# Three reads of the attention bias move from the sync engine's DMA queue to GpSimd's

## The chip, the cores and the metric

The kernel runs on one core of a Trainium2 chip. Its time is the device time of one execution in microseconds (us). The engines are PE (TensorE, matrix products), DVE (VectorE), ACT (ScalarE), POOL (GpSimd) and SP (SyncE, which here only issues DMAs). Each engine takes its instructions in program order; they wait for one another through semaphores. A DMA is issued by an engine's queue, and it "lands" when its last byte is there and its semaphore says so.

## What is computed

An attention with a bias that depends on positions, then two MLP blocks. Only the bias matters here; cut from the reference:

```
B, H, S, D = 4, 8, 576, 64
rel = pos[:, None] - pos[None, :]
x = (log1p(abs(rel)) / log1p(maximum(pos[:, None], 1.0)))[..., None]
bias = maximum(x @ w1 + b1, 0.0) @ w2            # (S, S, H): the same for every batch
scores = scale * q @ k.T + bias.transpose(2, 0, 1)[None]
attn = exp(scores - max) / (sum + 1e-9)
out = attn @ v                                   # then the MLP blocks
```

The bias is a 576 x 576 matrix for each of the 8 heads; row i depends on |i - j| alone, apart from the divisor.

## The kernel before

**Stages.** The kernel first computes the bias of all heads (about the first 53 us), then does the attention in 16 units (`UNITS`: four pairs of heads times four batches, `hp` and `b`), then the MLP blocks.

**The bias stage.** A strip z is 16 rows of the bias for all 8 heads, so 128 partitions. There are 36 strips, done in the order `ORDER`: strips 16 to 23, then 8 to 15, then 0 to 7, then 24 to 35; y is the place in that order. For each strip, `units` makes four hidden tiles m from L (a relu of shifted and scaled logs; most on DVE at L335, some on ACT at L333), `sums` multiplies them with the weights on PE (L347), and `finish` writes the result with its mirror image into a tile o (ACT at L354, DVE at L356). `store` (L368) then sends o to a scratch buffer `scr` in DRAM, 591 numbers a row. Reading `scr` back with a row pitch that is shorter by one turns this into the bias matrix. Strips 0 to 23 go with one store each. Strips 24 to 35 go in groups of 3 and 1, for the first two heads only at first (the other heads follow in the attention); the second head's stores of strips 32 to 34 and 35 are issued from ACT, all others from SP.

**The reads.** `read(k)` loads rows 128k to 128k+127 of the first two heads from `scr` into the tile `bias`. For even k a row is put in a turned order, so `turned` takes two DMAs (L262 and L263); for odd k it is one (L376). `read(4)` loads the last 64 rows with two (L276). `READ` says after which place y each is issued: read 2 after y = 20, read 0 after y = 27, read 1 after y = 29, read 3 after y = 32, read 4 after y = 35. Read k needs strips 8k to 8k+7.

**Who uses them.** The first attention unit works on nine blocks of 128 rows in the order `FIRST`: add 0, add 1, add 2, add 5, add 3, add 6, add 4 (DVE, L714: scores plus bias, with the row minimum). Add n takes read n mod 5: add 0 and 5 read 0, add 1 and 6 read 1, add 2 read 2, add 3 read 3, add 4 read 4. S n is the score product on PE (L708), exp n on ACT (L728), T n the transposes on PE (L734), hi n and lo n their split on ACT (L117) and DVE (L120).

**POOL.** Between 5 us and 51 us POOL has nothing to do in this stage. Behind the bias stage stands a first, tiny copy (`GATE`, L114, into w), which waits for the last strip's hidden tile; then come the low half of K for the second head (kl), the split of the next unit's q, of v, and some fills.

**Semaphores of DMAs.** As built, every DMA from SP or ACT counts on one of eight semaphores, named DMAHW0 to DMAHW7 in the rows of the program below, and waits for the DMA that used the same one before it. Those issued from POOL count on DMASW0 and following.

Of the kernel before, what the change touches and what calls it, by code (L numbers as in the profile page):

```python
# [100 lines left out]
def block_kernel(  # L101
# [6 lines left out]
    act, dve, pool, pe, sp = nc.scalar, nc.vector, nc.gpsimd, nc.tensor, nc.sync  # L108
# [146 lines left out]
    def rows(h, i, n):  # L255

        f = 16 + h * PITCH + i * (H * PITCH - 1)
        return scr[f:f + n * (H * PITCH - 1)].rearrange("(r c) -> r c", r=n)[:, :2 * PITCH].rearrange("r (h j) -> r h j", h=2)[:, :, :S]

    def turned(dst, src):  # L260

        sp.dma_start(out=dst[..., 64:], in_=src[..., :512])  # L262
        sp.dma_start(out=dst[..., :64], in_=src[..., 512:])  # L263

    def load_bias(hp, z):

        if hp not in bias:
            new_bias(hp)
        if z < 2:
            t = bias[hp][:, 5 * z:5 * z + 4]  # L270
            src = rows(2 * hp, 0, 512)[:, z].rearrange("(n p) j -> p n j", p=128)
            turned(t[:, ::2], src[:, ::2])
            sp.dma_start(out=t[:, 1::2], in_=src[:, 1::2])
        else:
            for h in range(2):
                sp.dma_start(out=bias[hp][64 * h:64 * h + 64, 4], in_=rows(2 * hp, 512, 64)[:, h])  # L276
# [4 lines left out]
    with ExitStack() as c:  # L281
# [21 lines left out]
        for f in (load_q, load_k):  # L303
# [9 lines left out]
            out=W.rearrange("p (g h) -> p g h", h=8), in0=w8.unsqueeze(1).to_broadcast([128, 4, 8]), in1=ind.unsqueeze(2).to_broadcast([128, 4, 8]), op=ALU.mult,  # L313
# [56 lines left out]
        def read(k):  # L370
            if k == 4:
                load_bias(0, 2)
                return
            t, src = bias[0][:, k::5], rows(0, 128 * k, 128)
            if k % 2:
                sp.dma_start(out=t, in_=src)  # L376
            else:
                turned(t, src)

        def finish(z, pts):  # L380
            l, r, n = reach(z)
            if z < FULL:
                t = stg.tile([128, 591], F32, name="o")
            else:
                if z % 4 == 0:
                    spare[z // 4] = M["spare"].tile([128, 4 * 591], F32, name="o")
                t = spare[z // 4][:, 591 * (z % 4):][:, :591]
            left, right = t[:, :l + 1][:, ::-1], t[:, l:]
            for o, pt in pts:
                scaled(EV[ORDER.index(z)][0], z, (right if z < 18 else left)[:, o], pt)  # L390
            if z < 18:
                scaled(EV[ORDER.index(z)][1], z, left[:, 1:], pts[0][1][:, 1:l + 1])
            else:
                scaled(EV[ORDER.index(z)][1], z, right[:, 1:], pts[0][1][:, 1:r])
            if z < FULL:
                store(z, 1, t)
            else:

                for n, at in GROUPS:
                    if z % 4 == at:  # L400
                        for h in range(2):
                            store(z + 1 - n, n, spare[z // 4][:, 591 * (at + 1 - n):591 * (at + 1)], h)
                if z % 4 == 3:
                    M.setdefault("held", []).append(lambda: store(z - 3, 4, spare[z // 4]))
            for k in READ.get(ORDER.index(z), ()):
                read(k)
# [5 lines left out]
        for y, z in enumerate(ORDER):  # L412
# [19 lines left out]
            if y == QK[2]:  # L432

                KH, KL = (qkp.tile([128, 2, S + 64], F32R, name=n) for n in ("kh", "kl"))
                k = raw[0].pop("k")
# [549 lines left out]
    def T_groups(b):  # L985
        return [g_T(b, j) for j in ([4] if b % 2 == 0 else []) + [0, 1, 2, 3]]
# [4 lines left out]
    with ExitStack() as c:  # L991
# [98 lines left out]
        for k in range(4):  # L1090
            for m in range(3):
                src = wiv[:, k, 1024 * m:1024 * m + 1024] if m < 2 else wov[:, k]
# [263 lines left out]
    t = {b: T_groups(b) for b in range(1, B)}  # L1356
# [83 lines left out]
```

## Time and profile before

| | us |
|---|---|
| median of 3 runs | 946.3 (946.25 to 948.57) |
| the profiled execution's own time | 945.16 |
| its span, first to last instruction | 943.4 |
| PE busy in the span | 922.5 (98%) |
| DVE busy | 720.6 (76%) |
| ACT busy | 494.9 (52%) |
| POOL busy | 425.1 (45%) |

The time is that of one core. PE is busy for nearly the whole span, so the stretches in which it isn't are where anything else can count: the bias stage and the first attention unit, in the first 70 us. Of the views, the chain of waits is the work that ended last, followed back from the end; the timeline shows instructions in order of time, with the idle time of the engine before one in brackets and what ended it; the table by stretches gives each engine's busy time in one.

### The profile page before, as it was taken

The numbers are of one execution on the slowest core, as the hardware profiler recorded it, in microseconds if no ns is written. First come the engines' busy times: TensorE is split into PE (matmuls) and PEld (weight loads), VectorE is DVE, ScalarE is ACT, GpSimd is POOL, SyncE is SP. The second block draws the span as 40 slices with busy tenths as digits, with TensorE's granted clock in tenths as the row PEclk, the third lists the DMA queues.
The fourth block names the chain that finished last, engine by engine and source line by source line (L and its number), as shares of the span: only waits on it lengthen the run. The fifth ranks groups of instructions, "written<-read, shape, count | busy, mean of one in ns | idle before, by whom it ended". The sixth has DMA issues, their size and how long they took to land.

```text
span 943.4 us, 16015 instructions
## 1 busy us (share of the span) xinstructions
PE 922.5 (98%) x5681; PEld 805.8 (85%) x5681; DVE 720.6 (76%) x1433; ACT 494.9 (52%) x1108; POOL 425.1 (45%) x555
## 2 busy tenths in 40 slices
PE   7889999999999999999999999999999999999998
PEld 2269999999999888888888888888888998989996
DVE  7988999999889687885779798979765656455452
ACT  8979999999998754322222222223132635253340
POOL 0068788978999543332224333433300524133251
PEclk9999999999999999999999999999999999999999
DMA  6878847757563561212122333233222000001001
GB/s 230 283 234 258 270 137 214 236 162 226 158 206 85 177 196 31 70 33 89 61 68 92 123 99 122 88 124 99 101 67 104 23 1 23 24 0 58 1 34 67
DMA packets 57983, 110.23 MB, mean 117 GB/s; under 512 B 10032, under 2 KB 21040, under 8 KB 57648
## 3 DMA queue, kind: packets, MB, share of 16 engines
q1 hardware_dynamic: 57504, 108.64, 36.1%
q8 instruction: 45, 0.74, 0.3%
q10 hardware_dynamic: 400, 0.58, 0.2%
q14 instruction: 34, 0.28, 0.1%
HBM read 71.37 MB, written 28.38 MB: 106 GB/s over the span
## 4 chain that ended last, share of the span: by engine, by line
PE 91%; DVE 5%; POOL 1%; DMA 1%; issue 1%; ACT 1%; DVEq 0%; SPq 0%; POOLq 0%; ACTq 0%
PE psh L124 21%; PE psy L124 21%; PE psa L124 10%; PE s L708 8%; PE PB L797 8%; PE psa L1284 6%; PE pt L734 6%; PE psa L1266 5%; DVE m L335 4%; PE pt L487 1%; PE OB L803 1%; PE s L744 1%; PE pt L347 1%; DVE ct L714 0%; DMA L<-in_c_log_dram 0%
## 5 line engine op out<-in xcount | busy, mean ns | idle before, releaser
L124 PE MATMUL psh<-blk,w1h 128*128 128x512 f32 (+1 forms) x640 | 151.5, 368 | 0.0
L176 POOL TENSOR_TENSOR cvl<-cvl,cvt 128x512 f32<-128x512 f32 x44 | 56.9, 1293 | 206.6 <-DVE cvt L173 179.0
L655 ACT ACTIVATE hh<-psh 128x512 fp32r<-128x512 f32 (+1 forms) x80 | 44.1, 553 | 194.4 <-PE psh L124 193.2
L124 PEld LDWEIGHTS psh<-blk,w1h 128*128 128x128 f32 x640 | 113.3, 188 | 20.8 <-DVE blk L120 0.2
L714 DVE CUSTOM_DVE_ANT_0 ct<-s,bias 128x576 f32<-128x576 f32 x144 | 107.0, 752 | 16.6 <-PE s L708 7.1
L728 ACT ACTIVATE a<-ct,sm 128x576 f32<-128x576 f32 x144 | 112.2, 779 | 3.2 <-DVE sm L714 2.6
L1087 DVE TENSOR_TENSOR x_sb<-psy,x_sb 128x512 f32<-128x512 f32 x144 | 97.2, 683 | 9.1 <-PE psy L124 8.6
L656 DVE SCALAR_TENSOR_TENSOR hl<-psh,hh 128x512 fp32r<-128x512 f32 (+1 forms) x80 | 50.5, 632 | 56.5 <-ACT hh L655 56.5
L124 PE MATMUL psy<-w2h,hh 128*128 128x512 f32 x288 | 90.2, 394 | 0.1
L124 PE MATMUL psy<-w2l,hh 128*128 128x512 f32 x288 | 88.9, 390 | 0.0
L124 PE MATMUL psy<-w2h,hl 128*128 128x512 f32 x288 | 88.8, 389 | 0.0
L734 PE MATMUL pt<-ident,a 128*128 128x128 f32 x576 | 84.9, 273 | 0.3 <-DVE at0l L120 0.3
L124 PE MATMUL psh<-blk,w1l 128*128 128x512 f32 (+1 forms) x320 | 79.0, 368 | 0.0
L708 PE MATMUL s<-kh,q 128*128 128x288 f32 x320 | 72.0, 314 | 3.1 <-DVE sm L714 2.4
L734 PEld LDWEIGHTS pt<-ident,a 128*128 128x128 f32 x576 | 68.6, 141 | 1.1 <-DVE at0l L120 0.6
L708 PE MATMUL s<-kl,q 128*128 128x288 f32 x320 | 65.8, 295 | 0.0
L124 PEld LDWEIGHTS psh<-blk,w1l 128*128 128x128 f32 x320 | 56.8, 189 | 10.0
L124 PEld LDWEIGHTS psy<-w2l,hh 128*128 128x128 f32 x288 | 54.0, 188 | 11.5
L124 PEld LDWEIGHTS psy<-w2h,hl 128*128 128x128 f32 x288 | 54.0, 188 | 11.5
L177 POOL TENSOR_TENSOR cvw<-cvl,cvw 128x512 f32<-128x512 f32 x44 | 59.9, 1362 | 3.5
L124 PEld LDWEIGHTS psy<-w2h,hh 128*128 128x128 f32 x288 | 52.6, 188 | 9.9 <-issue 0.2
L120 DVE TENSOR_TENSOR at0l<-pt,at0h 128x512 fp32r<-128x512 f32 (+1 forms) x80 | 49.5, 619 | 5.6 <-ACT at0h L117 5.2
(202 smaller groups left out, 2173.5 us busy)
## 6 DMA issues: line engine op xcount, KB each, us to landing
r<-in_moe_w_ch_dram SPq DMA_DIRECT2D x32, 512.0 KB, 4.8
k<-in_k_dram SPq DMA_DIRECT2D x16, 640.0 KB, 5.4
q<-q SPq DMA_DIRECT2D x64, 144.0 KB, 2.7
scr<-o SPq DMA_DIRECT2D x24, 295.5 KB, 3.3
v<-in_v_dram SPq DMA_DIRECT2D x16, 384.0 KB, 3.5
q<-in_q_dram SPq DMA_DIRECT2D x16, 288.0 KB, 3.7
bias<-scr SPq DMA_DIRECT2D x8, 576.0 KB, 5.7
bias<-scr SPq DMA_DIRECT2D x8, 512.0 KB, 5.0
```

The source lines that it names most:

```text
L120: (eng or dve).tensor_tensor(out=o, in0=i, in1=hi.bitcast(F32), op=ALU.subtract)
L124: pe.matmul(ps, lhsT=w, rhs=x, start=start and j == 0, stop=stop and j == len(terms) - 1)
L176: pool.tensor_tensor(out=T["l"], in0=T["l"], in1=T["t"].bitcast(F32), op=ALU.mult)
L177: pool.tensor_tensor(out=T["w"], in0=T["l"], in1=T["w"], op=ALU.add)
L656: dve.scalar_tensor_tensor(out=hl[:, f, :n], in0=ps[:, :n], scalar=0.0, in1=hh[:, f, :n].bitcast(F32), op0=ALU.max, op1=ALU.subtract)
L708: pe.matmul(s[:, x, :288], lhsT=w, rhs=m[:, 288 * x:288 * x + 288], start=j == 0, stop=j == len(prs) - 1)
L714: dve.tensor_tensor_reduce(out=ct, in0=s[:, :, :288], in1=bias[UNITS[u][0]][:, n].rearrange("p (a b) -> p a b", a=2), scale=-0.125, scalar ...
L728: act.activation(weights(n), ct.rearrange("p a b -> p (a b)"), AF.Exp, scale=-1.0, bias=mt, accum_out=SU[u % 2][:, n:n + 1])
L734: pe.transpose(PA[k % 2][:, j], e[:, 128 * j:128 * j + 128], ident)
L797: pe.matmul(d, lhsT=w, rhs=m, start=q == 0, stop=q == len(terms) - 1)
L1087: dve.tensor_tensor(out=x_sb[:, t], in0=ps, in1=x_sb[:, t], op=ALU.add)
L1284: pe.matmul(ps[:, z, :288], lhsT=v, rhs=w[:, 288 * z:288 * z + 288], start=(q == 0), stop=(q == len(terms) - 1))
```

## The change

`turned` takes the queue as an argument, and `read` hands POOL's queue to reads 0, 1 and 2 and SP's to read 3. Read 4 goes through `load_bias` and stays on SP. The later loads of bias, which call `turned` too, keep SP.

```diff
-    def turned(dst, src):
+    def turned(dst, src, q=sp):
-        sp.dma_start(out=dst[..., 64:], in_=src[..., :512])
-        sp.dma_start(out=dst[..., :64], in_=src[..., 512:])
+        q.dma_start(out=dst[..., 64:], in_=src[..., :512])
+        q.dma_start(out=dst[..., :64], in_=src[..., 512:])
...
             t, src = bias[0][:, k::5], rows(0, 128 * k, 128)
+            q = pool if k < 3 else sp
             if k % 2:
-                sp.dma_start(out=t, in_=src)
+                q.dma_start(out=t, in_=src)
             else:
-                turned(t, src)
+                turned(t, src, q)
```

What this does to the order, in two places. First POOL's queue, after its opening fills (L318): the five DMAs of reads 2, 0 and 1, in that order, ahead of the copy of the gate (into w) and of kl.

```order
 L318 MEMSET q_100 128x64
 L318 MEMSET q_101 128x64
+L262 DMA bias<-scr 128x2x512 [waits DMAHW5_49,DMAHW6_49,DMAHW3_49,DMAHW7_49,DMAHW1_49,DMAHW0_49]
+L263 DMA bias<-scr 128x2x64
+L262 DMA bias<-scr 128x2x512 [waits DMAHW4_49,DMAHW3_49,DMAHW5_49,DMAHW2_49,DMAHW7_49,DMAHW1_49,DMAHW0_49]
+L263 DMA bias<-scr 128x2x64
+L378 DMA bias<-scr 128x2x576
 L114 TENSOR_SCALAR w_141<-m 128x1 [waits DVE_49,Activation_49]
```

Read 2 now waits by itself for the stores of strips 16 to 23, read 0 for those of strips 0 to 7, and all that POOL does later stands behind them.

Second, SP's queue at the end of the bias stage. Before: read 0 (L262, L263), read 1 (L376), the stores of strips 28 to 30 and 31 for two heads, read 3 (L376), the first head's stores of strips 32 to 35, read 4 (L276).

```order
L262 DMA bias<-scr 128x2x512 [waits DMAHW6_49,DMAHW7_49,DMAHW5_49,DMAHW4_49]
L263 DMA bias<-scr 128x2x64
L376 DMA bias<-scr 128x2x576
L368 DMA scr<-o 16x3x591 [waits DMAHW0_49,Activation_49]
L368 DMA scr<-o 16x3x591 [waits DMAHW2_49]
L368 DMA scr<-o 16x591 [waits DMAHW3_49,Activation_49]
L368 DMA scr<-o 16x591 [waits DMAHW4_49]
L376 DMA bias<-scr 128x2x576 [waits DMAHW3_49,DMAHW4_49,DMAHW2_49,DMAHW5_49,DMAHW1_49,DMAHW0_49]
L368 DMA scr<-o 16x3x591 [waits DMAHW6_49,DVE_49,Activation_49]
L368 DMA scr<-o 16x591 [waits DMAHW7_49,DVE_49,Activation_49]
L276 DMA bias<-scr 64x576 [waits DMAHW7_49,DMAHW6_49,DMAHW1_49]
```

The same place now (L378 is read 3):

```order
L368 DMA scr<-o 16x3x591 [waits DMAHW2_49,Activation_49]
L368 DMA scr<-o 16x3x591 [waits DMAHW4_49]
L368 DMA scr<-o 16x591 [waits DMAHW5_49,Activation_49]
L368 DMA scr<-o 16x591 [waits DMAHW7_49]
L378 DMA bias<-scr 128x2x576 [waits DMAHW5_49,DMAHW4_49,DMAHW6_49,DMAHW2_49,DMAHW7_49,DMAHW1_49,DMAHW0_49]
L368 DMA scr<-o 16x3x591 [waits DVE_49,Activation_49]
L368 DMA scr<-o 16x591 [waits DVE_49,Activation_49]
L276 DMA bias<-scr 64x576 [waits DMAHW3_49,DMAHW6_49,DMAHW2_49,DMAHW1_49]
```

With five DMAs gone from SP, the eight semaphores fall to other DMAs, and read 3's list is another one. On ACT's queue, the two stores of the second head (strips 32 to 34, and 35) change theirs too:

```order
 L354 ACTIVATE o<-pt,small 128x280 [waits PE_49] x2
 L354 ACTIVATE o<-pt,small 128x31
-L368 DMA scr<-o 16x3x591 [waits DMAHW5_49,DVE_49,Activation_49]
+L368 DMA scr<-o 16x3x591 [waits DMAHW3_49,DVE_49,Activation_49]
 L354 ACTIVATE o<-pt,small 128x15 [waits DVE_49]
-L368 DMA scr<-o 16x591 [waits DMAHW1_49,DVE_49,Activation_49]
+L368 DMA scr<-o 16x591 [waits DMAHW6_49,DVE_49,Activation_49]
```

The first of them moved from DMAHW5, which is on read 3's list before, to DMAHW3, which is not on it now; the second from DMAHW1 to DMAHW6.

## Rows read from the trace of the kernel before

**Rows 1.** The page, chain that ended last: shares of the span by engine.
```profile
PE 91%; DVE 5%; POOL 1%; DMA 1%; issue 1%; ACT 1%; DVEq 0%; SPq 0%; POOLq 0%; ACTq 0%
```

**Rows 2.** Stretches: length, busy us of PE, PEld, DVE, ACT, POOL; clock; DMA.
```profile
58.00:60.00 2.00, 0.66 (x5) 0.58 (x5) 1.40 (x4) 1.34 (x3) 1.64 (x8) 1.00 0.07 26
60.00:65.00 5.00, 3.30 (x24) 2.63 (x23) 4.22 (x10) 3.46 (x9) 4.83 (x5) 1.00 0.86 234
...
70.00:80.00 10.00, 9.99 (x81) 9.75 (x80) 8.01 (x20) 9.01 (x24) 5.61 (x7) 1.00 0.84 257
```

**Rows 3.** Chain of waits, 36 to 63 us: start, length, what.
```profile
38.20 10.32 DVE m L335 x27
...
52.09 2.31 DMA scr<-o
...
54.48 3.96 DMA bias<-scr
```

**Rows 4.** Issues into bias, first 70 us: ns shortest/median/longest, first and last.
```profile
L262 SPq DMA_DIRECT2D bias<-scr x2: 449/644/838, 35.6 to 45.0; - x2
L263 SPq DMA_DIRECT2D bias<-scr x2: 462/710/957, 36.4 to 45.5; - x2
L376 SPq DMA_DIRECT2D bias<-scr x2: 360/415/470, 46.0 to 54.5; - x2
```

**Rows 5.** Waits of SP's queue, 36 to 60 us: total us, times, longest.
```profile
SPq L368 <- ACT o L354: 3.2, 4, 2.2
SPq L276 <- DMA scr<-o: 2.8, 1, 2.8
SPq L368 <- ACT m L333: 1.3, 1, 1.3
```

**Rows 6.** DMA issues, 44.9 to 46.6 us: count, KB each, us to landing.
```profile
bias<-scr SPq DMA_DIRECT2D x1, 576.0 KB, 5.6
bias<-scr SPq DMA_DIRECT2D x1, 512.0 KB, 3.9
bias<-scr SPq DMA_DIRECT2D x1, 64.0 KB, 3.6
```

**Rows 7.** DMA issues, 46.6 to 54.9 us.
```profile
scr<-o SPq DMA_DIRECT2D x2, 36.9 KB, 4.0
scr<-o ACTq DMA_DIRECT2D x1, 36.9 KB, 1.8
```

**Rows 8.** DMA issue of the last store of strips 0 to 7, at 39.56 us.
```profile
scr<-o SPq DMA_DIRECT2D x1, 295.5 KB, 5.3
```

**Rows 9.** Timeline of DVE, 50.3 to 58.8 us: start, length, what, [idle before].
```profile
53.22 0.76 DVE L714 CUSTOM_DVE_ANT_0 ct<-s,bias 128x576 f32<-128x576 f32 x1 [0.36 <-DMA scr<-o]
...
53.90 0.75 DVE L714 CUSTOM_DVE_ANT_0 ct<-s,bias 128x576 f32<-128x576 f32 x1
...
58.60 0.76 DVE L714 CUSTOM_DVE_ANT_0 ct<-s,bias 128x576 f32<-128x576 f32 x1 [1.29 <-DMA bias<-scr]
```

**Rows 10.** Timeline of all engines, 57.2 to 62.7 us: two rows of ACT.
```profile
59.40 0.78 ACT L728 ACTIVATE a<-ct,sm 128x576 f32<-128x576 f32 x1 [0.66 <-DVE sm L714]
...
61.22 0.61 ACT L117 ACTIVATE at1h<-pt 128x512 fp32r<-128x512 f32 x1 [0.47 <-PE pt L734]
```

**Rows 11.** Timeline of POOL, 50.9 to 60 us.
```profile
50.99 0.19 POOL L114 TENSOR_SCALAR w<-m 128x1 f32<-128x1 f32 x1 [46.00 <-ACT o L354]
...
55.72 1.84 POOL L120 TENSOR_TENSOR v<-v,v 128x768 fp32r<-128x768 f32 x1
```

**Rows 12.** All instructions of L161, in the MLP's weight conversion: ns shortest/median/longest.
```profile
L161 DVE TENSOR_SCALAR cvt<-r x44: 393/420/1486, 90.1 to 667.6; 128x512 int32<-128x512 int32 x44
```

**Rows 13.** Timeline of DVE, 376.5 to 381 us.
```profile
378.25 1.49 DVE L161 TENSOR_SCALAR cvt<-r 128x512 int32<-128x512 int32 x1
```

**Rows 14.** Timeline of POOL, the same stretch.
```profile
378.17 1.29 POOL L177 TENSOR_TENSOR cvw<-cvl,cvw 128x512 f32<-128x512 f32 x1
```

**Rows 15.** All instructions of L817, a small operation of POOL: ns shortest/median/longest.
```profile
L817 POOL TENSOR_SCALAR sm<-sm x16: 198/200/419, 75.7 to 313.9; 128x9 f32<-128x9 f32 x16
```

## The prediction

> **What bounds the kernel now.** I read the page's chain first: 91% of it is PE [rows 1]. The table by stretches says where PE is not yet the bound: it is busy 9.99 of 10 us from 70 us on, but 0.66 of 2 from 58 us and 3.30 of 5 from 60 us [rows 2]. So a microsecond won or lost before that arrives at the end, and PE has only 1.34 + 1.70 = 3.0 us there to win. The chain of waits for those microseconds has two parts before the attention runs freely [rows 3]. Through the last third of the bias stage it is DVE's hidden tiles, back to back (27 of them in 10.32 us from 38.20, and a few more after). Then a store of 2.31 us from 52.09 holds read 3, whose own 3.96 us from 54.48 hold add 3. DVE idles 1.29 us for read 3 [rows 9]; that wait is what this change can touch.
>
> **What the change removes from SP.** Five issues: two of L262 (median 0.644), two of L263 (0.710) and the first of L376, the longer one (0.470), 2 x 0.644 + 2 x 0.710 + 0.470 = 3.2 us of SP's queue [rows 4]. By itself this is worth nothing. Behind read 2 the next store waits 1.3 us for ACT anyway, and the four other waits of stores in that stretch, 3.2 us in all, are for ACT's tiles too [rows 5]: SP is ahead of the bias stage, not behind it.
>
> **What it removes from read 3.** Two things. First, read 3 needs strips 24 to 31, but the chain holds it behind the store issued from ACT at 52.09, which is strips 32 to 34. The order shows how: that store counts on DMAHW5, and DMAHW5 is on read 3's list. In the changed program the store counts on DMAHW3, which isn't on the list. So read 3 waits for the stores of strip 31 alone. Second, those stores landed 4.0 us after their issue, while the one of the same size from ACT took 1.8 [rows 7]: on SP they queued behind 1.15 MB of reads 0 and 1 [rows 6]. Issued as before, the last of them (49.57) landed at about 53.4; with 1.8 us it would be 51.4. Read 3 then goes out between 51.4 and 53.4 instead of 54.48 and, at the same 3.96 us, lands between 55.4 and 57.4. DVE is free for add 3 at 58.60 - 1.29 = 57.31 [rows 9]. I take the whole 1.29 us as gone.
>
> What is late next? PE's products after add 3 start 1.29 us earlier. But ACT had waited only 0.66 us for add 3, so its row of work to at1h, which had 0.47 us of idle time left before 61.22, reaches at1h at 61.22 - 0.47 - 0.66 = 60.1 [rows 10]. That is **1.1 us** earlier, and I carry that. Read 4 stood behind read 3 in SP's queue and waited 2.8 us for stores that were issued after it [rows 5]; these move up with read 3, so it doesn't become the next wait.
>
> **What it adds to POOL.** Five issues. The trace of before shows no DMA on POOL's queue, so their length is bounded: at least 0.36 us, SP's shortest issue [rows 4], at most 1.84 us, POOL's longest operation near there [rows 11]. POOL is idle for 46 us until 50.99 [rows 11], and the strips that read 2 needs are the first eight of the stage, so read 2 costs nothing. Reads 0 and 1 wait for the last store of strips 0 to 7, issued at 39.56 and landed 5.3 us later, at 44.9 [rows 8]. Add 0 starts at 53.22 and add 1 at 53.90 [rows 9]. With landings of 3.6 and 5.6 us [rows 6], read 0's second DMA has to be issued by 49.6 and read 1's by 48.3. That leaves 3.4 us for the two issues ahead of read 1's, 1.7 us each. I take an issue like SP's 0.47 to 0.96, so the cover holds: zero. The copy at 50.99 isn't delayed either.
>
> **What it may add to DVE.** This is the term that I can't read directly. DVE's hidden tiles go from SBUF to SBUF as a scalar operation of one tensor, and the same kind in the weight conversion (L161) takes 0.42 us in the median and up to 1.49 [rows 12]. The long one at 378.25 ends when POOL's operation from 378.17 to 379.46 has ended [rows 13, 14]: the two took turns. If a DMA's issue on POOL holds DVE up in this way, it hits the part of the chain that has no slack. Below, zero: nothing holds. Above, 1.49 - 0.42 = 1.07 us an issue, 5.4 us for five. I take 0.20 us an issue, the length of POOL's small operations [rows 15], since an issue streams no tensor through POOL: 5 x 0.20 = **1.0 us** added.
>
> **Sum.** 945.16 - 1.1 + 1.0 = 945.1 for the profiled execution. The median of the runs is 946.3, 1.14 above that execution, so **946.2**. With no hold-up of DVE it is 945.2; with 2 us of it 947.2. That is the forecast's own range. About 0.3%, 2.8 us, is what a measurement of this kernel can tell from no change, so this is no change.
>
> **The rivals.**
>
> *POOL's issues can't get through while DVE streams (slower).* DVE streams its hidden tiles back to back until just before POOL's copy at 50.99, which waits for the last of them [rows 3, 11]. If POOL is the one that has to wait in the taking of turns, the issues of reads 0 and 1 are done only after that. Three issues from 50.8 at 0.47 to 1.29 us each [rows 4, 14] put the start of read 1's DMA at 51.7 to 53.4; with at least 4 us to landing add 1 starts at 55.7 to 58 instead of 53.90, 1.8 to 4.1 us late. Read 3 is not waited for then, so 1.29 us come back: +0.5 to +2.8. If read 2's two issues are stuck as well, another 0.9 to 2.6 us: up to +5.4. In the middle +3, **949.3**. It decides from the point where read 1's issue starts after 49. For it: the taking of turns is in the rows. Against: operations of both engines got through in the weight conversion within one operation of the other. The Trainium skill, "SBUF — State Buffer", section "Who interferes with whom", has this as its rule: a DMA stalled by a DVE operation was one issued from GpSimd, whose descriptor writing doesn't get the port it shares with DVE. The section on the bandwidth-pool intuition gives 620 ns alone and 3100 ns beside a DVE copy; by my estimate from that factor of five, three issues of 0.47 us would take 2.4 us each, read 1's would start at 49.6 and land at 55.2, add 1 would be 1.3 us late, which add 3's lost wait pays for, and the sum would be about 946.3. No run here shows it yet. Chance 0.22.
>
> *POOL holds DVE for whole operations (slower).* The same turns the other way: three quarters of the 1.07 bound, 0.8 us, five times is 4.0, less 1.1: +2.9, **949.2**. For it: the 1.49 us of L161. Against: those were tensor operations of 1.3 us. Chance 0.15.
>
> *The reads crowd the stores as before (the change does not bring read 3 forward).* Reads 0 and 1 start at about the same time as they did, from another queue, and share the same DMA engines. Then read 3 waits as long, and the 1.0 us on DVE remains: **947.3**. Against: one of its two waits is gone from the list whatever the DMAs do. Chance 0.08.
>
> *More than the one wait.* All of PE's 3.0 us of idle time from 58 to 65 us closes, since read 4 and the placing of the next unit's q stand in the same queue, and DVE isn't held: 946.3 - 3.0 = **943.3**. Against: DVE is busy 4.22 of the 5 us from 60, ACT 3.46 [rows 2], so engines limit PE there more than DMAs do. Chance 0.05.
>
> **How the numbers follow.** Forecast 0.50, rivals 0.22, 0.15, 0.08 and 0.05. Slower by over 0.3% means above 949.1: about half of the first rival and somewhat over half of the second, 0.20. Faster means below 943.5: most of the last, 0.03. Within: 0.77. The range must hold eight in ten: from 944.7, half a microsecond under the forecast without any hold-up, to 950.6, which takes in the first two rivals but for the case with all five issues stuck.
>
> **What would show it.** Right: the DVE row of add 3 without its 1.29 us of idle time, read 3 issued before 53.5, the chain up to the last hidden tile longer by about 1 us, hidden tiles of over 0.6 us at the five issues on POOL. Starved issues would show as add 0 or add 1 waiting for DMA, with POOL's copy later than 50.99. Wrong in size: if the bias stage ends 3 us later, POOL holds DVE for whole operations; if it ends at the same time, not at all. I would be wrong altogether if the first DMA on POOL's queue costs something that no row shows, or if the other order of semaphores puts a false wait elsewhere.

## The result, and the profile after

The change made the kernel slower. The median is 953.45 us (953.27 to 954.29, four runs) against 946.73 (946.25 to 948.57, four runs) beside it: a ratio of 1.0072, with a 95% interval of 1.0058 to 1.0085, or **6.7 us more**. The forecast was 946.2, "no change". The profiled execution took 953.27 us, with a span of 951.5 against 943.4 before, so 8.1 more. Of these 7.0 are there by the first units of the attention, at 69 us, and still 7.0 at the attention's last add (316.35 against 309.37); the last 1.1 us come behind the attention. One execution of the kernel with only read 2 on POOL, the one that has its trace, took 1147.7 us at a granted clock of 0.75; its figures below leave that one out.

In the changed program L262 and L263 keep their numbers, and everything below is two lines further down: L376 is now L378, the adds are L716, S is L710. First POOL's timeline from 20 to 53 us (start, length, engine, line, what, and in brackets the idle time before and what ended it); a DMA here is the time that its issue takes the engine.

```profile
21.84 0.96 POOL L262 DMA_DIRECT2D bias<-scr  x1 [16.21 <-DMA scr<-o]
22.80 0.73 POOL L263 DMA_DIRECT2D bias<-scr  x1
44.38 6.91 POOL L262 DMA_DIRECT2D bias<-scr  x1 [20.84 <-DMA scr<-o]
51.29 0.72 POOL L263 DMA_DIRECT2D bias<-scr  x1
52.00 0.72 POOL L378 DMA_DIRECT2D bias<-scr  x1
52.76 0.20 POOL L114 TENSOR_SCALAR w<-m 128x1 f32<-128x1 f32 x1
```

Four of the five issues take 0.7 to 1.0 us, as an issue of SP's does [rows 4]. The third, read 0's first, takes **6.91 us**, from 44.38 to 51.29. What DVE does in that time stands in its timeline from 43.9 to 65 us:

```profile
43.69 7.45 DVE L335 TENSOR_SCALAR m<-L,shift 128x496 f32<-128x496 f32 x18
...
56.95 0.76 DVE L716 CUSTOM_DVE_ANT_0 ct<-s,bias 128x576 f32<-128x576 f32 x1 [3.78 <-DMA bias<-scr]
...
59.93 0.76 DVE L716 CUSTOM_DVE_ANT_0 ct<-s,bias 128x576 f32<-128x576 f32 x1 [2.21 <-DMA bias<-scr]
...
64.21 0.75 DVE L716 CUSTOM_DVE_ANT_0 ct<-s,bias 128x576 f32<-128x576 f32 x1
...
```

Eighteen hidden tiles run back to back until 43.69 + 7.45 = 51.14; each starts some 0.08 us before the one ahead has ended, so that there is no gap in the row. POOL's issue ends 0.15 us behind the last of them. DVE isn't much slower for it: before, its last hidden tile ended at 49.89 + 0.94 = 50.83, and the experiments show below that the same tiles take the same time with such issues and without. It is POOL that waits for DVE, and not the other way about. DVE's timeline before:

```profile
49.89 0.94 DVE L335 TENSOR_SCALAR m<-L,shift 128x576 f32<-128x576 f32 x2
```

What follows from it is in the same rows. Add 0 waits 3.78 us for its read and comes at 56.95 instead of 53.22 (+3.7), add 1 waits again and comes at 59.93 instead of 53.90 (+6.0) [rows 9]. Add 3 no longer waits for read 3: its row has no bracket where that of before had 1.29 [rows 9], and it is 5.6 us late. The DMA issues of 51 to 54 us (count, KB, us from the start of the issue to landing):

```profile
bias<-scr POOLq DMA_DIRECT2D x1, 576.0 KB, 7.8
...
bias<-scr POOLq DMA_DIRECT2D x1, 64.0 KB, 5.5
```

Read 1 needs 7.8 us where it needed 5.6, the small part of read 0 5.5 where it needed 3.6 [rows 6]; read 3, which SP now issues at 51.49, falls into the same microseconds. Last, the table by stretches (length, busy us of PE, PEld, DVE, ACT, POOL, then the granted clock, DMA share, GB/s):

```profile
54.00:56.00 2.00, 0.09 (x1) 0.00 (x0) 0.00 (x0) 0.00 (x0) 1.92 (x3) 1.00 1.04 331
56.00:58.00 2.00, 0.23 (x1) 0.23 (x2) 0.77 (x2) 0.25 (x1) 1.92 (x3) 0.58 0.96 364
58.00:60.00 2.00, 1.10 (x4) 0.75 (x4) 0.07 (x1) 0.62 (x2) 1.85 (x6) 0.50 0.22 84
...
64.00:66.00 2.00, 2.00 (x11) 1.98 (x10) 1.55 (x4) 0.96 (x4) 2.00 (x2) 0.50 0.96 261
66.00:68.00 2.00, 2.00 (x16) 1.98 (x14) 1.07 (x4) 2.00 (x6) 1.92 (x2) 0.86 1.03 396
```

PE is busy 0.32 of 4 us while it waits for add 0. Then the granted clock falls to 0.50, its lower level of 1.2 GHz, and comes back only after PE has been busy again. That adds to the first loss. Before, the clock was 1.00 over the stretches shown from 58 us on [rows 2].

### The profile page after: what moved, and what is told of

Read it like the earlier page. It is cut to its first block, busy times and chain, and to the rows that moved or that the text cites. A ratio compares the mean times of both kernels' runs of the same rounds, so it can differ in the third digit from the quotient of the medians.

```text
span 951.5 us, 16031 instructions
## 1 busy us (share of the span) xinstructions
PE 926.4 (97%) x5681; PEld 808.9 (85%) x5681; DVE 720.9 (76%) x1433; ACT 495.2 (52%) x1108; POOL 435.0 (46%) x560
## 5 line engine op out<-in xcount | busy, mean ns | idle before, releaser
L716 DVE CUSTOM_DVE_ANT_0 ct<-s,bias 128x576 f32<-128x576 f32 x144 | 107.0, 752 | 21.8 <-PE s L710 8.2
L710 PE MATMUL s<-kh,q 128*128 128x288 f32 x320 | 73.2, 319 | 6.2 <-DVE sm L716 5.5
L710 PE MATMUL s<-kl,q 128*128 128x288 f32 x320 | 66.9, 299 | 0.0
L710 PEld LDWEIGHTS s<-kh,q 128*128 128x128 f32 x320 | 50.1, 193 | 8.6 <-DVE sm L716 6.6
```

The costliest lines, as they stand in the source:

```text
L710: pe.matmul(s[:, x, :288], lhsT=w, rhs=m[:, 288 * x:288 * x + 288], start=j == 0, stop=j == len(prs) - 1)
L716: dve.tensor_tensor_reduce(out=ct, in0=s[:, :, :288], in1=bias[UNITS[u][0]][:, n].rearrange("p (a b) -> p a b", a=2), scale=-0.125, scalar ...
```

## The experiments

Theory A was formed from these rows: **an issue of POOL's doesn't get through while DVE runs its hidden tiles back to back**, and passes 0.15 us behind the last one of such a row, or beside another kind of DVE instruction. One issue in the same traces doesn't fit it; the last section has it. Its rivals: the 6.91 us are the issue's own (D); DMAs from POOL hold DVE up (B); the lateness is contention of the reads and not the issue (C, G). The ratios below are to the kernel before, run on the same chip.

### Only read 2, and only read 0, on POOL

```diff
-            q = pool if k < 3 else sp
+            q = pool if k == 2 else sp
```

> Only read 2 goes to POOL; reads 0 and 1 stay on SP, as before. Theory A (POOL's issue is held only where DVE streams its hidden tiles back to back, and what cost the 6.7 us of the full change is read 0's first issue, 6.91 us long): read 2's issues fall beside the low half of K on DVE and take about 1 us each, as in the full change; adds 0 and 1 come where they came before. Time 945 to 947.5, so 0.99 to 1.001 of before. Rival B (any DMA from POOL during the bias stage holds up DVE's tiles, by some 0.3 us or more an issue): DVE's last hidden tile ends later than 50.8 and the time is 947.5 to 949.

Measured: 946.06 us against 947.07, ratio 0.9988 (0.9977 to 0.9998). Read 2 on POOL costs nothing, and gains about a microsecond (0.2 to 2.2 by the interval). In its trace read 2's two issues take 0.96 and 0.73 us, as A said. B's price, 947.5 or more, is outside.

```diff
-            q = pool if k < 3 else sp
+            q = pool if k == 0 else sp
```

> Only read 0 goes to POOL; reads 2 and 1 stay on SP. Theory A: read 0's first issue starts at about 44.4, is held until DVE's last hidden tile has ended (51.1), and its data lands at 55 to 56.5; add 0 is 2.3 to 3.7 us later than before. Read 1 comes from SP by 51, so add 1 follows add 0 at once. Time 948.5 to 951. Rival C (the late issue costs little by itself; three reads of 576 KB at the same time made the landings long): only reads 0 and 3 meet, read 0 lands within 4 us of its issue, add 0 is under 2 us late, and the time is 946.5 to 948.

Measured: 950.47 against 947.07, ratio 1.0035 (1.0022 to 1.0047), so 3.4 us more. POOL's timeline, then DVE's:

```profile
47.94 3.73 POOL L262 DMA_DIRECT2D bias<-scr  x1 [42.87 <-DMA scr<-o]
```

```profile
49.73 1.80 DVE L335 TENSOR_SCALAR m<-L,shift 128x560 f32<-128x560 f32 x4
...
57.57 0.76 DVE L716 CUSTOM_DVE_ANT_0 ct<-s,bias 128x576 f32<-128x576 f32 x1 [4.01 <-DMA bias<-scr]
...
58.26 0.75 DVE L716 CUSTOM_DVE_ANT_0 ct<-s,bias 128x576 f32<-128x576 f32 x1
```

Here POOL came to the issue 3.6 us later (its stores landed later in this execution), and yet the issue ends at the same point, at 51.67, 0.14 behind the last hidden tile (49.73 + 1.80 = 51.53). So its end doesn't hang on when it starts, but on DVE. Add 0 is 4.35 us late, more than the 2.3 to 3.7 that A gave (the whole bias stage ended 0.7 us later in this execution), and add 1 follows at once, as A said. C's 946.5 to 948 is outside. Half of the 6.7 us is read 0 alone.

### Another kind of DVE instruction for four or six hidden tiles

```diff
+                    if ORDER.index(z) == 31:
+                        dve.scalar_tensor_tensor(out=m, in0=L[:, :n], scalar=shift[:, k], in1=zero[:, :1].to_broadcast([128, n]), op0=ALU.add, op1=ALU.max)
+                    else:
                         dve.tensor_scalar(out=m, in0=L[:, :n], scalar1=shift[:, k], scalar2=0.0, op0=ALU.add, op1=ALU.max)
```

> The full change, and the four hidden tiles of strip 31 on DVE (about 44.5 to 46.1 us) are computed by a scalar-tensor-tensor operation with a zero as the third operand, the same result by another kind of DVE instruction, some 0.2 us longer each. Theory A: DVE's tensor-scalar tiles are what holds POOL's issue, so that read 0's first issue ends inside these four tiles, at 45 to 47 us instead of 51.3; read 0 lands by 51, add 0 is not late, and read 1 either gets in too (time 946.5 to 948.5) or waits for the next opening at 51 (time 948 to 951). Rival D (the 6.91 us are the issue's own: its waits, the ring of its queue, the descriptors): it still takes 6 to 7 us, and the time is 953.5 to 955.

Lines are one to four further down in this kernel: L263, L264 and L382 are the issues. POOL's timeline, then DVE's:

```profile
44.55 0.72 POOL L263 DMA_DIRECT2D bias<-scr  x1 [20.93 <-DMA scr<-o]
45.27 0.72 POOL L264 DMA_DIRECT2D bias<-scr  x1
45.99 0.72 POOL L382 DMA_DIRECT2D bias<-scr  x1
```

```profile
44.23 2.73 DVE L337 SCALAR_TENSOR_TENSOR m<-L,shift,zero 128x512 f32<-128x512 f32 x4
46.88 5.09 DVE L339 TENSOR_SCALAR m<-L,shift 128x528 f32<-128x528 f32 x12
...
55.12 0.76 DVE L720 CUSTOM_DVE_ANT_0 ct<-s,bias 128x576 f32<-128x576 f32 x1 [0.38 <-ACT o L358]
...
55.80 0.75 DVE L720 CUSTOM_DVE_ANT_0 ct<-s,bias 128x576 f32<-128x576 f32 x1
```

The issue that took 6.91 us takes 0.72, and all three pass beside the four changed tiles. Neither add 0 nor add 1 waits for a read. D falls: nothing of POOL's queue, of the semaphores or of the transfers was changed, only the kind of four DVE instructions. The median is 948.08 against 947.07, ratio 1.0026 (1.0008 to 1.0044). But the twelve times spread: eight from 946.2 to 948.7, four from 950.3 to 954.5. For what is left there are two more kernels: the same edit in the kernel before, and the full change with six such tiles (`in (31, 32)`).

> The kernel before, with the four hidden tiles of strip 31 on DVE by the three-operand instruction: a control for the price of that alone. Each of the four took 0.66 us from start to start where the others take 0.40, so that the hidden tiles end 1.07 us later; the time is 947.5 to 948.5 against some 946.8 of before, 1.0008 to 1.0015. If the full change with this edit (1.0026, 1.0008 to 1.0044) is no slower than this control, nothing of the 6.7 us is left once the issues get through; if it is slower by over 1.5 us, something of the loss hangs on other things than the held issue.

Measured: 946.50 against 946.52, ratio 1.0002 (0.9994 to 1.0011). The four tiles take 2.73 us in this kernel too, in place of some 1.6, and add 0 comes later; but add 3's wait for read 3 takes most of that up, 0.38 us of idle time before it (and that for PE) in place of 1.29 [rows 9]. So the control costs less than the 0.8 to 1.5 per mille that was expected. From DVE's timeline:

```profile
44.85 2.73 DVE L337 SCALAR_TENSOR_TENSOR m<-L,shift,zero 128x512 f32<-128x512 f32 x4
47.50 5.09 DVE L339 TENSOR_SCALAR m<-L,shift 128x528 f32<-128x528 f32 x12
...
54.97 0.76 DVE L718 CUSTOM_DVE_ANT_0 ct<-s,bias 128x576 f32<-128x576 f32 x1 [0.35 <-DMA scr<-o]
...
59.47 0.76 DVE L718 CUSTOM_DVE_ANT_0 ct<-s,bias 128x576 f32<-128x576 f32 x1 [0.38 <-PE s L748]
```

With the issues let through, add 0 of the full change (55.12) stands 0.15 us from that of the control (54.97), and at the attention's last add it is 0.17 us ahead (310.00 against 310.17): in that execution nothing of the loss is left there. Its span is still 1.4 us longer (945.7 against 944.3), which comes behind the attention, where nine traces of kernels with DMAs from POOL, with held issues or without, need 634.6 to 636.2 us from that add to the end, and those of before and of the control 634.0 and 634.1; why was not followed. The same rows settle B, too: the four tiles take 2.73 us and the twelve after them 5.09 with POOL's three issues beside the four and without, so DVE loses nothing to an issue there.

> The full change with the hidden tiles of strips 31 and 32 on DVE (six) by the three-operand instruction, in place of those of strip 31 alone. The single times of that kernel with four lay between 946.2 and 954.5, eight of twelve under 949; Theory A puts the high ones down to executions in which POOL came to its first issue so late that the second or third missed the four tiles and waited for 51 us. Then the opening, now some 4.7 us long, takes all three in every execution: all times within 946.5 to 950, the median at 947.5 to 949. Rival: the high times have another cause (the state of DMA queues, the clock), and they stay, up to 952 or more.

Measured: 948.20 against 946.52, ratio 1.0018 (1.0009 to 1.0026), the twelve times from 946.85 to 950.57. The high ones are gone (three of twelve lay above 951 with four tiles), as A has it, though one lies above the 950 that it allowed. That the four high times of the kernel with four tiles were executions in which POOL came too late for the opening is argued from this; no trace of one was taken. The two further slow tiles cost 0.54 us, and the rest of the 1.7 isn't accounted for.

### Short instructions with a PSUM operand as openings

```diff
-    AA AA AA AA AA AA AA AA AD DD AA DA
+    AA AA AA AA AD AD AD AA AD DD AA DA
```

(The table of who writes the two halves of each strip; second letter D: the second half goes from ACT to DVE.)

> The full change, and the second halves of the writes of strips 28, 29 and 30 (127, 111 and 95 columns out of PSUM) go from ACT to DVE, so that DVE has three short instructions with a PSUM operand between its hidden tiles, at about 46.1, 47.1 and 48.8 us. Theory A (the issue is held by the back-to-back tiles whose operands all lie in SBUF, and passes at any other DVE instruction): read 0's two issues and read 1's end at about 46.3, 47.2 and 48.9 or earlier, adds 0 and 1 are not late, the last hidden tile is 0.6 us later, and with read 3 no longer waiting the time is 945 to 947.5. Rival I (such a short instruction is no opening, and the zero-operand tiles let the issues in for another reason, their length): read 0's first issue still ends after 51, and the time is 953 to 954.5.

Measured: 948.17 against 946.62, ratio 1.0017 (1.0005 to 1.0029), more than the expected 945 to 947.5. POOL's timeline, then DVE's:

```profile
48.18 0.72 POOL L262 DMA_DIRECT2D bias<-scr  x1 [24.13 <-DMA scr<-o]
48.90 1.78 POOL L263 DMA_DIRECT2D bias<-scr  x1
50.67 2.78 POOL L378 DMA_DIRECT2D bias<-scr  x1
```

```profile
48.54 0.34 DVE L356 TENSOR_SCALAR o<-pt,small 128x111 f32<-128x111 f32 x1
48.78 1.74 DVE L335 TENSOR_SCALAR m<-L,shift 128x544 f32<-128x544 f32 x4
50.43 0.32 DVE L356 TENSOR_SCALAR o<-pt,small 128x95 f32<-128x95 f32 x1
50.66 2.64 DVE L335 TENSOR_SCALAR m<-L,shift 128x560 f32<-128x560 f32 x6
```

This is the closest view of the mechanism. The first issue passes beside the 111 columns. The second starts at 48.90, between hidden tiles, and ends at 50.68, 0.16 behind the last of four (48.78 + 1.74). The third starts at 50.67 and ends at 53.45, 0.15 behind the last of six (53.30). Rival I falls: a DVE instruction of 0.32 us is an opening. But an opening lets only those through that are there: in this execution POOL came to read 0 at 48.18, when the first of the three openings had passed, read 1 missed the last one, and add 1 was late. (With 950.57 us it is the second slowest of the twelve.)

### The opening of read 2 moved away, and read 1 sent early

```diff
-                split_lo(KL[:, 0], k[:, 0], KH[:, 0])
+            if y == 14:
+                split_lo(KL[:, 0], k[:, 0], KH[:, 0])
```

> The full change with the low half of K for the first head (DVE, 0.8 us, two operands) three places later, at about 26 us instead of 21.7. Theory A: read 2's first issue, which passed beside it in 0.96 us, is now held from 21.8 until the next such opening, so that it takes 2 us or more and ends at 24 to 27 us; nothing else moves, and the time is that of the full change, 953 to 954.5. Rival D (the issue's length has nothing to do with what DVE runs): read 2's first issue takes about 1 us again.

Measured: 953.48 in one run. POOL's timeline, then DVE's:

```profile
22.50 3.14 POOL L262 DMA_DIRECT2D bias<-scr  x1 [16.81 <-DMA scr<-o]
```

```profile
24.24 1.25 DVE L335 TENSOR_SCALAR m<-L,shift 128x336 f32<-128x336 f32 x3
25.41 0.82 DVE L120 TENSOR_TENSOR kl<-k,kh 128x640 fp32r<-128x640 f32 x1
```

Read 2's issue, 0.96 us long before the edit, now takes 3.14 and ends at 25.64, 0.15 behind the hidden tile ahead of kl (25.49). It had passed at once in the full change because kl happened to be beside it.

```diff
-READ = {20: [2], 27: [0], 29: [1], 32: [3], 35: [4]}
+READ = {20: [2, 1], 27: [0], 32: [3], 35: [4]}
...
-            q = pool if k < 3 else sp
+            q = pool if k in (1, 2) else sp
```

> Reads 2 and 1 go to POOL, both right after place 20, where read 2 alone stood; read 0 goes to SP. Theory A: read 1's issue follows read 2's second one and either gets through in the same opening (by 25 us) or waits for the next one, which costs nothing as long as it lands by 53; three of SP's issues are saved, and SP's stores of strips 28 to 31 and read 3 are earlier. Time 944.5 to 946.5, 0.998 to 1.000 of before. Rival B (DMAs from POOL hold up DVE): 947.5 or more. If read 1's issue is held to 51 us as read 0's was, add 1 is late by 2 to 4 us: 948 to 951.

Measured: 945.83 against 947.07, ratio 0.9987 (0.9976 to 0.9997): 1.2 us less than before, if barely outside no change. Read 1's issue is held here too, 4.74 us, and ends 0.14 behind a hidden tile (38.11 + 0.78 = 38.89), beside a PSUM instruction; POOL's timeline, then DVE's:

```profile
34.29 4.74 POOL L378 DMA_DIRECT2D bias<-scr  x1 [10.21 <-DMA q<-q]
```

```profile
38.11 0.78 DVE L335 TENSOR_SCALAR m<-L,shift 128x416 f32<-128x416 f32 x2
38.80 0.33 DVE L356 TENSOR_SCALAR o<-pt,small 128x111 f32<-128x111 f32 x1
...
58.09 0.75 DVE L716 CUSTOM_DVE_ANT_0 ct<-s,bias 128x576 f32<-128x576 f32 x1
```

Held or not, nobody waits for it, because 15 us are left. And add 3 (58.09) doesn't wait for read 3, although the bias stage ended later in this execution (add 0 at 54.06): the wait that the prediction wanted gone is gone, and nothing else is late.

### What a late issue costs: contention and the clock

`no3` sends read 3 early, with rows that are there already, so that its rows of the bias are others:

```diff
-            t, src = bias[0][:, k::5], rows(0, 128 * k, 128)
+            t, src = bias[0][:, k::5], rows(0, 128 * (2 if k == 3 else k), 128)
...
-READ = {20: [2], 27: [0], 29: [1], 32: [3], 35: [4]}
+READ = {20: [2, 3], 27: [0], 29: [1], 35: [4]}
```

> The full change with read 3 taken out of the meeting of the reads: it is sent right after place 20 and reads rows 256 to 383 once more (so that its rows of the bias are not those of the reference; its size is the same). Theory G (a part of the lateness of adds 0 and 1 is that reads 0, 1 and 3 share the DMA engines at 52 to 59 us): read 0, issued until 52.0, lands within 4 us, read 1 by 57.5; add 0 comes at 55 to 56 instead of 56.95, add 1 at 56.5 to 58 instead of 59.93, and the time is 949.5 to 952. Rival H (the landing of a read of that size takes 5 us or more after a late issue, whatever else runs): add 0 stays at 56.5 or later, add 1 at 59 or later, and the time is 952.5 to 954.

Measured: 952.78 against 946.62, ratio 1.0056 (1.0034 to 1.0078). From DVE's timeline, and the DMA issues of 51 to 54 us:

```profile
55.97 0.76 DVE L716 CUSTOM_DVE_ANT_0 ct<-s,bias 128x576 f32<-128x576 f32 x1 [2.66 <-DMA bias<-scr]
...
58.88 0.76 DVE L716 CUSTOM_DVE_ANT_0 ct<-s,bias 128x576 f32<-128x576 f32 x1 [2.15 <-DMA bias<-scr]
```

```profile
bias<-scr POOLq DMA_DIRECT2D x1, 576.0 KB, 6.6
```

Adds 0 and 1 come 1.0 us earlier than in the full change: add 0 (55.97) is within G's bound of 56, add 1 (58.88) is between G's 58 and H's 59, and the time is above G's range (949.5 to 952) and within H's. So neither holds as it stood. Contention with read 3 makes about 1 us of add 1's 6.0, going by one execution of each kernel, and the time has a gain of 0.7 or 1.5 (by the medians or by the ratios) that the interval doesn't separate from none. Read 1 needs over 6 us without read 3 too, and it needed 6.0 in the kernel with four other tiles, whose issues weren't held and whose read 3 went out only after both had landed: most of the length is not read 3's doing.

`warm` gives PE something to do while it waits, 22 products into a tile that nobody reads:

```diff
+        kh = ops[0][1][:, 0]
         for w in FIRST:
             name, *args = w.split()
+            for _ in range({"S 2": 16, "S 5": 6}.get(w, 0)):
+                pe.matmul(PT[0], lhsT=kh[:, :128], rhs=kh[:, :512].rearrange("p (a b) -> p a b", a=4), start=True, stop=True)
```

> The full change, and 22 matrix products into an unused PSUM tile, 16 after S 1 and 6 after S 2, where PE stood idle for 3.7 and 1.7 us: PE stays busy while add 0 and add 1 wait for their reads. Theory E (part of the 6.7 us is the granted clock, which fell to 0.50 over 58 to 66 us after PE's idling): the clock stays at 1.00 over 54 to 68 us, the chain S 5, T 0, S 3, T 1 runs as fast as before, and the time is 951 to 952.5, some 1 to 2.5 us under the full change's 953.4. Rival F (PE is not what the first unit waits for there; the reads alone set it): the clock stays up and the time is 953 to 954.

Measured: 951.39 (950.48 to 952.13) against 946.62, ratio 1.0047 (1.0032 to 1.0062), against the full change's 1.0072: some 2 us back, for no useful work. The table by stretches:

```profile
56.00:58.00 2.00, 2.00 (x11) 1.68 (x10) 0.77 (x2) 0.87 (x2) 1.92 (x3) 1.00 0.95 314
58.00:60.00 2.00, 2.00 (x13) 1.75 (x13) 1.44 (x4) 0.87 (x2) 1.93 (x4) 1.00 0.63 243
```

The clock stays at 1.00, as E said, and F's 953 to 954 is outside. The size is not clean: the profiled execution is the fastest of the six. In it read 3 happened to go out later (53.91), and add 1 came at 58.05 and not at 59.93. That is earlier than without read 3 (58.88), so the landings vary by other things as well. And the filler itself ran past the point where S 2 and S 5 could have started. What can be read behind add 1 is how late the second split of the first units (at1l, on DVE) comes: before, in the full change, and here:

```profile
61.92 0.69 DVE L120 TENSOR_TENSOR at1l<-pt,at1h 128x512 fp32r<-128x512 f32 x1 [0.44 <-ACT at1h L117]
```

```profile
68.94 0.69 DVE L120 TENSOR_TENSOR at1l<-pt,at1h 128x512 fp32r<-128x512 f32 x1
```

```profile
65.55 0.68 DVE L120 TENSOR_TENSOR at1l<-pt,at1h 128x512 fp32r<-128x512 f32 x1
```

From add 1 to at1l the full change loses another 1.0 us (at1l is 7.0 late, its add 1 6.0), although it saves add 3's 1.29; with the clock up, at1l is 3.6 late where add 1 is 4.2, so that 0.5 is won. By these two executions the clock is worth about 1.5 us of the 6.7, as an estimate.

## Why the prediction was wrong

**The step that failed is "so the cover holds: zero"**, the term for POOL's issues. Each was priced as an issue of SP's, 0.47 to 0.96 us. That is right for an issue that isn't held (0.72 to 0.96), and the points from which it would cost something stand: read 0's second DMA by 49.6, read 1's by 48.3. But read 0's first issue was held for 6.91 us, so that its second one began at 51.29 and read 1's at 52.00, 1.7 and 3.7 us behind these points. The term was not 0 but what became of it: add 1 6.0 us late.

**The choice between the cases.** The first rival, with a chance of 0.22, named this mechanism, the place (until the last hidden tile), and the sign to look for (add 0 and add 1 waiting for DMA, POOL's copy after 50.99: it is at 52.76). It was put behind the forecast because operations of both engines had got through in the weight conversion within one operation of the other [rows 13, 14]. Those rows didn't bear on this case: there POOL's operation had begun first (378.17), and one operation of DVE's (378.25) ended late beside it. Here eighteen stood in a row, each starting before the one ahead had ended, and in five executions shown above the issue ended 0.14 to 0.16 us behind the last one of such a row, whether it had begun 1.8, 2.8, 3.1, 3.7, 4.7 or 6.9 us earlier. Read 0's first issues in the traces of `late_kl`, `no3` and `warm`, held for 5.2, 5.5 and 6.1 us, end the same way. The Trainium skill, "SBUF — State Buffer", section "A bandwidth-pool intuition that's wrong (but worth ruling out)", says that such a DMA is blocked until the end of the DVE operation plus some 115 ns; the traces agree in kind, with 0.14 to 0.16 us measured, if the end is that of the whole row of tiles. The rival took from that page the factor of five between its two times and multiplied, which gave 2.4 us an issue, where the page says that such a multiplication is the wrong model. By the same page's section "Who interferes with whom", copies and scalar operations can take the port that both share for their whole length, and an operation with two tensors lets a DMA's issue through (the page calls the reason inferred). The traces agree, but for read 2's second issue (last section): the issues of 0.72 to 0.96 us passed beside kl and the four changed tiles, and beside instructions that read PSUM.

**The rival's price.** It gave +0.5 to +2.8, at most +5.4 with read 2 stuck too. The measured 6.7, with read 2 not stuck, has three terms that it lacked. It took "at least 4 us" for read 1's landing, though the row for that read says 5.6 [rows 6], and 7.8 were needed. (Its upper end of 58 for add 1 doesn't follow from 53.4 and 4 us either, which give 57.4.) It had no contention, though read 3, sent 3.0 us earlier by the other half of the argument, had to meet the late reads (about 1 us). And it had no clock: it was read as 1.00 [rows 2], and what a wait of 4 us does to it was not asked (about 1.5 us).

**What was right.** Read 3 did go out earlier, at 51.49 instead of 54.48, at the early end of the range of 51.4 to 53.4; the timeline of SP's queue in the changed kernel has it:

```profile
51.49 0.39 SPq L378 DMA_DIRECT2D bias<-scr  x1
```

The stores of strip 31 ahead of it landed 1.9 us after their issue instead of 4.0 [rows 7], as was argued, and add 3's 1.29 us were gone. Of the DMA issues from 47 to 50.2 us:

```profile
scr<-o SPq DMA_DIRECT2D x2, 36.9 KB, 1.9
```

With two reads on POOL where nobody waits for them, the time is 1.2 us less (0.3 to 2.3 by the interval), against the 1.1 carried. That this is read 3's gain alone is not shown: the kernel with only read 2 on POOL gained 1.0 us as well, with reads 0 and 1 still on SP. So it isn't shown either that SP's 3.2 us of issues are worth nothing by themselves.

**The hold-up of DVE** was put at +1.0, from 0 to 5.4. It is nought within what can be seen: DVE's last hidden tile ends at 51.14 against 50.83, and where the same tiles can be compared with three issues and without, they take the same 2.73 and 5.09 us. The second rival falls with it. The third (the reads crowd the stores) fell with the stores' 1.9 us and read 3's earlier issue, the fourth with the sign of the result.

**What stays open.** The span of the profiled execution grew by 8.1 us, the median by 6.7; the last 1.1 us of the span come behind the attention and were not followed, so it is open whether some of the 6.7 belongs there. How the 6.7 divides is known only roughly: about half is read 0 alone (3.4 measured), the rest read 1, with some 1 us of contention and 1.5 of the clock in both, these two from one execution of each kernel. And one kind of issue was not held, as the last section says.

## What to carry to other kernels

Before a DMA is moved to GpSimd's queue, look at what DVE runs at the moment when the issue becomes ready: beside a row of scalar operations of one tensor from SBUF to SBUF it can wait for the end of the whole row, not for one of them, and a single operation with two tensors or with a PSUM operand was enough to let one issue through. Such an issue belongs where its data are needed long after the next opening. And price a wait by all that hangs on it: the transfers that now meet, and PE's clock if PE has nothing else to do.

## What was not expected of the hardware

The hold seems to hang on a short part of POOL's issue, for it passed beside an instruction of 0.32 us and ended some 0.15 us after a row of tiles. And there is an exception to the rule of the row that no experiment here explains. Read 2's second issue in the full change ran from 22.80 to 23.53 (first fence of the result), when kl had ended (22.55) and the hidden tiles were back to back again, and it was not held. Here DVE gave way instead: one tile beside it took 0.53 us where the one ahead had taken 0.39. DVE's timeline there:

```profile
21.74 0.81 DVE L120 TENSOR_TENSOR kl<-k,kh 128x640 fp32r<-128x640 f32 x1
...
22.86 0.39 DVE L335 TENSOR_SCALAR m<-L,shift 128x352 f32<-128x352 f32 x1
23.17 0.53 DVE L335 TENSOR_SCALAR m<-L,shift 128x352 f32<-128x352 f32 x1
```

The same issue passes in the same way in the traces of `hole`, `hole2`, `early12`, `no3` and `warm`. That it comes right behind an issue that had just got through doesn't explain it, since in `open_ev` read 0's second issue came so, too, and was held. What is shown is that an issue that reached a row of hidden tiles was held to its end nine times, in seven traces, and that this one was not, in six.
